# Batch 1 of a fused windowed-attention and feed-forward kernel split into two token groups, with the order of its loads, the trigger of w_out's last quarter and one attention group's key changed

## Chip, cores and metric

One core of one Trainium2 chip. The metric is the device time of one execution in microseconds (us), of the slowest core (here the only one). The four executions of the kernel before lie within 0.5% (229.15 to 230.26 us). A run is marked slow when it is over 1.5% above the fastest of its kernel; ratios use the other, "fast" runs alone. Profiles are of single executions; their span is about 1.7 us shorter than the time (229.87 against 228.2).

## The reference

```python
# q, k, v: (4, 8, 768, 64) = batch, heads, tokens, head size; n_sink = 4, window = 128
scores = q @ k.T / 8
keep   = (key < 4) | ((0 <= query - key) & (query - key < 128))
a      = softmax(where(keep, scores, -1e9))
x      = (a @ v), heads side by side            # (3072, 512)
g      = relu(x @ w_in) ** 2                    # w_in (512, 2048)
out    = g @ w_out                              # w_out (2048, 512)
```

So each batch has attention over a window of 128 keys plus 4 "sink" keys, and then two matrix products, called layer 1 and layer 2 here.

## The kernel before

The kernel plans itself: each operation has a key and a cost, a small planner in the program estimates start times and fixes one order for each engine; on the chip every engine runs its program in that order. What the change and the argument touch:

```python
sizes = dict(att=2, den=2, qr=5, qs=6, vf=3, expm=8, r=3, osb=2)   # buffers; att, den: PSUM
GROUPS = {b: [(0, 6)] for b in range(B)}            # first token, tiles of 128 tokens
GROUPS[0] = [(0, 2), (256, 2), (512, 2)]

def load_qk(b, m0, ti, g, ...):                     # on the SP queue: 4 heads of q or k
    ... in_=(q, k)[ti][b, 2*m0:2*m0+4, t0:t0+128*n, :].rearrange("h (p t) d -> p h (t d)", t=n)

# VectorE (or GpSimd): the four sink rows of v, spread over the heads; from 8 KB "vs_in"
def sink_values(e):
    for j in range(NP):
        tensor_tensor(out=vs[32*j:32*j+32, 2*j:2*j+2, :], in0=vs_in[:, b:b+1, :]..., op=mult)
# values (PE): needs the masks, the cast v tiles and sink_values; takes a PSUM buffer
# norm (VectorE): reciprocal and multiply out of that PSUM buffer, which is free after it
# layer1 (PE): takes a "den" buffer; relu (ACT), square (VectorE)
# layer2 of batch 0, tokens 0 to 511: goes through w_out by quarters and keeps both
#   "den" buffers until the fourth quarter is done
# attention of batch 0 and 1 may use both "att" and "den"

# order of the loads, from batch 1 on; load_w_out and the loads of batch 2 are on the POOL queue
for m0 in (0, 2):
    for ti in (1, 0):
        load_qk(1, m0, ti, 0, ...)                  # 4 x 768 KB
load_w_out(3, ("qk", 1, 0, 0, 0), ...)              # behind the first q load
for s in range(NS):
    load_v(1, s, ...)                               # 3 x 2 x 256 KB
for b in range(1, B):
    load_sinks("sp", b)                             # 8 KB each, last of all
# batch 2's first load waits for ("v", 1, 3), the fourth of batch 1's six v loads

at(2, 0.8, 1.3, "att")                              # batch 0's last attention group
attention(1, lambda f: -0.1 + 0.4 * f)(0, 0.0, 1.0, ("att", "den"))
```

The softmax here doesn't subtract the row's maximum and nothing guards it: scores larger than these inputs give would overflow.

Of the kernel before, what the change touches and what calls it, by code (L numbers as in the profile page):

```python
# [40 lines left out]
class Plan:  # L41
# [11 lines left out]
    def op(self, key, engines, run, after=(), takes=(), reads=(), dma=0.0, follow=()):  # L53
        o = Op(key, engines, run, after, takes, reads, dma, follow)
        self.ops.append(o)
        return o
# [77 lines left out]
def kernel(  # L134
# [17 lines left out]
    NS = NT // 2  # L152
# [127 lines left out]
    def dma_op(queue, name, run, us, behind=None, takes=(), yields=()):  # L280

        def go(e):
            ds = run(e)
            if behind is not None:
                for d in ds:
                    after_dma(d, loaded[behind])
            loaded[name] = ds[-1]
        o = op(-5, {queue: (0.85 if queue == "pool" else 0.5) + (0.3 if behind else 0.0)}, go, dma=us, takes=takes,
               follow=[chained[queue]] if queue in chained else (),
               after=[ops[behind]] if behind is not None else ())  # L290
        ops[name] = chained[queue] = o
        o.yields += [ops[y] for y in yields]
        o.follow += [ops[y] for y in yields]
        return o
# [9 lines left out]
    def load_w_out(i, behind=None, yields=()):  # L304
        w_out_op[i] = dma_op(
            "pool", ("w_out", i),
            lambda e: [nc.gpsimd.dma_start(
                out=w_out_sb[:, 4 * i:4 * i + 4, :],
                in_=moe_w_out[512 * i:512 * i + 512, :].rearrange("(p f) m -> p f m", p=128))],
            2.6, behind, yields=yields)  # L310
# [6 lines left out]

    GROUPS = {b: [(0, 6)] for b in range(B)}
    GROUPS[0] = [(0, 2), (256, 2), (512, 2)]
    ROW = {256: 0.0205, 512: 0.028, 1024: 0.046, 1536: 0.068}  # L320

    def load_qk(b, m0, ti, g, behind=None, yields=()):


        t0, n = GROUPS[b][g]
        half = (g if g < 2 else m0 // 2) if b == 0 else None
        share = (m0 if g < 2 else "g2", ti) if b == 0 else (b, m0, ti)
        if not half:
            qr_slot[share] = Slot("qr", 2)
        qr_slot[b, m0, ti, g] = qr_slot[share]  # L330

        def run(e):
            if b == 0:
                if half == 0:
                    qr_t[share] = work["qr"].tile([128, 2, 4, n * D], FP32, name="qr", tag="qr")
                t = qr_t[share][:, half]
            else:
                t = work["qr"].tile([128, 4, n * D], FP32, name="qr", tag="qr")
            qr_t[b, m0, ti, g] = t
            return [nc.sync.dma_start(  # L340
                out=t,
                in_=(q, k)[ti][b, 2 * m0:2 * m0 + 4, t0:t0 + 128 * n, :].rearrange(
                    "h (p t) d -> p h (t d)", t=n))]
        ops["qk", b, m0, ti, g] = dma_op("sp", ("qk", b, m0, ti, g), run, 32 * ROW[256 * n], behind,
                                         () if half else [qr_slot[share]], yields)

    def load_v(b, s, behind=None, yields=()):

        sl = vf_slot[b, s] = Slot("vf", 1)
        for i in range(2):  # L350
            t = 2 * s + i

            def run(e, i=i, t=t):
                if i == 0:
                    vf_t[b, s] = work["vf"].tile([128, 2, H, D], FP32, name="vf", tag="vf")
                return [nc.sync.dma_start(
                    out=vf_t[b, s][:, i], in_=v[b, :, 128 * t:128 * t + 128, :].rearrange("h p d -> p h d"))]
            dma_op("sp", ("v", b, t), run, 8 * 8 * ROW[256], behind if i == 0 else None,
                   [sl] if i == 0 else (), yields)
# [35 lines left out]
    def attention(b, key):  # L395
# [16 lines left out]
        def stage(g, f0, f1, side):  # L412

            t0, n = groups[g]
            last = t0 + 128 * n
# [6 lines left out]
            if b in NATURAL:  # L422
                for s in range(NS):
# [10 lines left out]
                            ops["turn", b, ti, t].margin = 4.0  # L434
                            copies.append(ops["turn", b, ti, t])
                    ops["cast", b, s] = ops["v", b, 2 * s + 1]
            w = 2 if b == 0 else 1
            for m in range(0, NP, w) if b not in NATURAL else ():
                f = 0.08 * m
                m0 = m - m % 2  # L440
# [245 lines left out]
    def layer1(b, key, fbs, c0, cw, need):  # L686
        n = len(fbs)
        xT = xT_sb[b % 2]
        bs, rs = Slot("den", 1), Slot("r", 1)
        tag = (b, fbs[0], c0)  # L690

        def mm(e):
            pm = bank_t[tag] = bank(bs, "pm", [128, n, cw], FP32)
            for i, fb in enumerate(fbs):
                for kb in range(NKB):
                    nc.tensor.matmul(pm[:, i, :], lhsT=w_in_sb[:, fb // 4, kb, fb % 4:512:4],  # L696
                                     rhs=xT[:, c0 // 256:(c0 + cw) // 256, kb, :], start=(kb == 0), stop=(kb == NKB - 1))
        a = op(key, {"pe": n * NKB * cw / 2380.0}, mm, takes=[bs],
               after=[ops["xT", b, s] for s in need] + [w_in_op[fbs[0] // 4]])
        ops["layer1", b, fbs[0], c0] = a  # L700

        def relu(e):
            r = bank_t[tag, "r"] = work["r"].tile([128, n, cw], BF16, name="r", tag="r")
            if e == "act":
                nc.scalar.activation(out=r, in_=bank_t.pop(tag), func=AF.Relu)  # L705
            else:
                nc.vector.tensor_scalar_max(r, bank_t.pop(tag), 0.0)
        ra = op(key, {"act": 0.19 + n * cw / 1200.0, "dve": 1.25}, relu, after=[a], takes=[rs], reads=[bs])

        def square(e):  # L710
            r = bank_t.pop((tag, "r"))
            (nc.vector if e == "dve" else nc.gpsimd).tensor_mul(  # L712
                gT_sb[c0 // 512][:, fbs[0]:fbs[0] + n, c0 % 512:c0 % 512 + cw], r, r)
        ops["sq", b, fbs[0], c0, cw] = op(key, {"dve": 0.7}, square, reads=[rs],
                                      after=[ra] + [ops[x] for x in ops if x[0] == "layer2" and x[1] == b - 1])
# [65 lines left out]
    for g, m0 in ((0, 0), (0, 2), (1, 0), (1, 2)):  # L781
        for ti in (1, 0):
            load_qk(0, m0, ti, g)
        if g:
            load_v(0, m0 // 2)
# [4 lines left out]
    for m0 in (0, 2):  # L790
        for ti in (1, 0):
            load_qk(0, m0, ti, 2, ("w_out", 0) if m0 == 0 and ti == 1 else None, [("w_out", 1)])
    load_v(0, 2)
    load_w_out(2, ("qk", 0, 2, 0, 2), [("v", 0, 5)])
    for m0 in (0, 2):
        for ti in (1, 0):
            load_qk(1, m0, ti, 0, ("qk", 0, 2, 0, 2) if m0 == 0 and ti == 1 else None, [("w_out", 2)])
    load_w_out(3, ("qk", 1, 0, 0, 0), [("qk", 1, 2, 0, 0)])
    for s in range(NS):
        load_v(1, s, yields=[("w_out", 3)] if s else ())  # L800
    for b in range(1, B):
        load_sinks("sp", b)

    LO, HI = 0.05, 0.6
    for b in range(B):
        if b == 0:
            at = attention(0, lambda f: f - 1.0)
            at(0, 0.0, 0.5, ("den", "att"))
            at(1, 0.5, 1.0, ("den", "att"))
            w_in_op[2].follow += [ops["cast", 0, 0]]  # L810
            w_out_op[0].follow += [ops["cast", 0, 1]]
            late["masks"] = op(-0.01, {"pool": 3.0}, build_masks, after=[c_tri, ops["bridge", 0, 1]])
            at(2, 0.8, 1.3, "att")
        if b == 0:
            for i in range(4):
                for s in range(2):
                    layer1(b, 0.083 * i + 0.042 * s, range(4 * i, 4 * i + 4), 256 * s, 256, (s,))
        else:
            for i, fb in enumerate(range(0, NFB, 2)):
                layer1(b, b + 0.333 * i / 8, (fb, fb + 1), 0, 512, (0, 1))  # L820
        for i, fb in enumerate(range(0, NFB, 4)):
            layer1(b, b + 0.333 + 0.167 * i / 4, range(fb, fb + 4), 512, 256, (2,))
        if b + 1 < B:
            if b + 1 in NATURAL:
                for s in range(NS):
                    load_natural(b + 1, s, [o for x, o in ops.items() if x[0] == "values" and x[1] == b - 1])
            attention(b + 1, (lambda f: -0.1 + 0.4 * f) if b == 0 else lambda f, b=b: b + LO + (HI - LO) * f)(
                0, 0.0, 1.0, ("att", "den") if b == 0 else "att")
        for u in range(NS):
            if b == 0 and u < 2:  # L830
                layer2(b, u, lambda i, part, u=u: 0.5 + 0.5 * (4 * part + 2 * u + i) / 24, by_part=True)
            else:
                layer2(b, u, lambda i, part, u=u, b=b: b + 0.5 + 0.5 * (8 * u + 4 * i + part) / 24)
# [36 lines left out]
```

## Time and profile before

| | before |
|---|---|
| time, median of the three first runs | 230.25 us |
| span of the profiled run | 228.2 us |
| TensorE (PE) busy | 216.7 us |
| PE idle 43.50 to 54.85 us | 2.73 us |
| PE idle 54.85 to 82.30 us | 1.20 us |
| batch 1's sink rows land | 58.80 us |

PE is the bound: all it does not do is 11.5 us. The prediction shows the lines for that. One more view matters later, VectorE's timeline (start, length, engine, line, operation, out<-in, shapes, count; in brackets the idle time before and who ended it):

```profile
59.06 0.70 DVE L208 CAST v<-vf 128x1024 bf16<-128x1024 f32 x1 [1.40 <-DMA vf<-in_v_dram]
59.67 2.37 DVE L519 TENSOR_TENSOR vs<-vs_in,head_rows 32x130 bf16<-32x130 f32 x8
62.16 0.69 DVE L712 TENSOR_TENSOR gT<-r 128x1024 bf16<-128x1024 bf16 x1
```

The second line is the work on the sink rows of batches 1 and 2. It has no bracket: the rows had landed 0.9 us before VectorE came to it.

### The profile page before, as it was taken

How to read it: one execution, taken by the hardware profiler on the slowest of the kernel's cores; microseconds unless marked ns; L12 is line 12 of the kernel's file. 1: busy time of each engine (PE TensorE's matmuls, PEld its weight loads, DVE VectorE, ACT ScalarE, POOL GpSimd, SP SyncE). 2: the span in 40 equal slices, each digit the busy share in tenths (PEclk: the TensorE clock that was granted, in tenths of full speed). 3: DMA queues.
4: the chain of work that ended last, by engine and by line, in shares of the span. 5: the costliest groups of instructions: out<-in, count | busy, mean ns of one | idle time of the engine just before them, and what ended most of it. 6: DMA issues, size and time to landing. Idle time of an engine off the chain costs nothing.

```text
span 228.2 us, 4562 instructions
## 1 busy us (share of the span) xinstructions
PE 216.7 (95%) x1923; PEld 138.2 (61%) x1940; DVE 105.3 (46%) x196; ACT 113.9 (50%) x127; POOL 56.4 (25%) x85
## 2 busy tenths in 40 slices
PE   7989999878999989999999999999999999999993
PEld 7558995455785665579545445488545455784441
DVE  6673444477775568575434015585532023440010
ACT  2496556344776478578260147768351056551010
POOL 5175016132986549766000000000000000000000
PEclk9999999999999999999999999999999999999999
DMA  5999989999999999999995630004061420000222
GB/s 158 269 201 206 215 207 261 309 320 218 174 197 142 141 201 137 142 123 146 156 138 152 174 115 3 0 0 49 0 122 38 120 95 0 0 0 3 92 94 92
DMA packets 84245, 29.70 MB, mean 130 GB/s; under 512 B 70272, under 2 KB 80768, under 8 KB 84224
## 3 DMA queue, kind: packets, MB, share of 16 engines
q0 software_dynamic: 40128, 8.92, 48.6%
q1 hardware_dynamic: 43912, 20.35, 41.2%
q8 instruction: 15, 0.25, 0.4%
q10 hardware_dynamic: 184, 0.14, 0.2%
q14 instruction: 6, 0.05, 0.1%
HBM read 27.30 MB, written 6.29 MB: 147 GB/s over the span
## 4 chain that ended last, share of the span: by engine, by line
PE 76%; DMA 10%; ACT 6%; DVE 4%; issue 1%; SPq 1%; ACTq 0%
PE pm L696 34%; PE py L736 32%; DMA qr<-in_q_dram 7%; PE po L636 5%; DMA w_out_sb<-in_moe_w_out_dram 4%; PE ps L575 4%; ACT r L705 4%; DVE gT L712 2%; ACT expm L594 1%; SPq L340 1%; PE px L673 1%; DVE qkT L208 1%; PE pk L535 1%; ACT qkT L206 1%; PE ps L568 0%
## 5 line engine op out<-in xcount | busy, mean ns | idle before, releaser
L696 PE MATMUL pm<-xT,w_in_sb 128*128 128x256 bf16 (+1 forms) x576 | 87.1, 309 | 0.5 <-ACT r L705 0.4
L736 PE MATMUL py<-w_out_sb,gT 128*128 128x512 bf16 x369 | 85.6, 379 | 2.0 <-DMA w_out_sb<-in_moe_w_out_dram 1.0
L696 PEld LDWEIGHTS <-w_in_sb 128*128 128x128 bf16 x576 | 62.7, 114 | 20.8 <-issue 2.1
L705 ACT ACTIVATE r<-pm 128x1024 bf16<-128x1024 f32 x48 | 49.3, 1027 | 32.2 <-PE pm L696 24.2
L736 PEld LDWEIGHTS <-gT 128*128 128x128 bf16 x384 | 36.1, 98 | 42.0 <-issue 2.4
L712 DVE TENSOR_TENSOR gT<-r 128x1024 bf16<-128x1024 bf16 x48 | 33.7, 701 | 55.3 <-ACT r L705 55.2
L594 ACT ACTIVATE expm<-ps 128x1024 bf16<-128x1024 f32 (+1 forms) x48 | 43.2, 955 | 12.5 <-PE ps L575 12.4
L206 ACT ACTIVATE osb<-py 128x1024 f32<-128x1024 f32 x11 | 11.3, 1025 | 45.4 <-PE py L736 45.4
L603 DVE TENSOR_TENSOR expm<-expm,mask 128x1024 bf16<-128x1024 bf16 (+1 forms) x38 | 25.0, 668 | 17.5 <-ACT expm L594 16.9
L636 PEld LDWEIGHTS <-expm 128*128 128x128 bf16 x352 | 16.5, 97 | 5.8 <-issue 1.8
L636 PE MATMUL po<-v,expm 128*128 128x65 bf16 x352 | 17.7, 193 | 2.0 <-DVE qkT L208 1.2
L648 DVE TENSOR_TENSOR xn_sb<-po,rc 128x512 bf16<-128x512 f32 x24 | 16.6, 691 | 1.1 <-DVE rc L647 0.3
L575 PE MATMUL ps<-qkT 64*128 64x128 bf16 (+1 forms) x256 | 14.8, 238 | 0.4 <-DVE xn_sb L648 0.2
L575 PEld LDWEIGHTS <-qkT 64*128 64x128 bf16 x256 | 8.0, 94 | 9.9 <-issue 8.0
L636 PE MATMUL po<-vs,es 128*128 128x65 bf16 x128 | 13.1, 193 | 0.0
L206 ACT ACTIVATE qkT<-pt 128x512 bf16<-128x512 bf16 (+1 forms) x11 | 7.2, 674 | 11.6 <-PE pt L472 9.8
L647 DVE RECIPROCAL rc<-po 128x8 f32<-128x8 f32 x24 | 4.9, 205 | 16.9 <-PE po L636 16.8
L210 POOL CAST qs<-qr 128x512 bf16<-128x512 f32 (+1 forms) x8 | 6.0, 750 | 24.2 <-DVE gT L712 12.3
L373 POOL DMA_DIRECT2D qn<-in_q_dram x12 | 10.8, 906 | 3.8 <-DMA qn<-in_k_dram 3.7
L636 PEld LDWEIGHTS <-es 128*128 128x128 bf16 x128 | 11.7, 97 | 0.0
L373 POOL DMA_DIRECT2D qn<-in_k_dram x12 | 10.7, 898 | 2.9 <-DMA vf<-in_v_dram 1.6
L383 POOL DMA_DIRECT2D v<-in_v_dram x12 | 10.6, 888 | 2.5 <-DMA qn<-in_q_dram 1.9
(50 smaller groups left out, 93.0 us busy)
## 6 DMA issues: line engine op xcount, KB each, us to landing
out_dram<-osb SPq DMA_DIRECT2D x11, 512.0 KB, 3.0
vf<-in_v_dram SPq DMA_DIRECT2D x12, 256.0 KB, 5.2
w_in_sb<-in_moe_w_in_dram POOLq DMA_DIRECT2D x4, 512.0 KB, 8.1
w_out_sb<-in_moe_w_out_dram POOLq DMA_DIRECT2D x4, 512.0 KB, 10.9
qr<-in_k_dram SPq DMA_DIRECT2D x6, 256.0 KB, 4.4
qr<-in_q_dram SPq DMA_DIRECT2D x6, 256.0 KB, 4.5
qr<-in_k_dram SPq DMA_DIRECT2D x2, 768.0 KB, 8.0
qr<-in_q_dram SPq DMA_DIRECT2D x2, 768.0 KB, 9.6
```

The lines of the kernel that those rows point to most:

```text
L206: nc.scalar.activation(out=dst, in_=src, func=AF.Copy)
L373: return [nc.gpsimd.dma_start(out=qn_t[b, ti][:, t, :].rearrange("p (h d) -> p h d", d=D), in_=(q, k)[ti][b, :, 128 * t:128 * t + 128, :]. ...
L383: return [nc.gpsimd.dma_start(out=v_sb[b % 2][:, t, :, 0:D], in_=v[b, :, 128 * t:128 * t + 128, :].rearrange("h p d -> p h d"))]
L575: nc.tensor.matmul(ps[:, h2, o:o + w], lhsT=qkT_sb[r, m, 1, c, :], rhs=qkT_sb[r, m, 0, qb:qb + w // 128, :], start=(i == 0 and not biased) ...
L594: nc.scalar.activation(out=x[:, :, o:512], in_=bank_t["s", b, s, m][:, :, o:512], func=AF.Exp, scale=scale)
L603: nc.vector.tensor_mul(x[:, :, o:512], x[:, :, o:512], mk[:, :, o:512])
L636: nc.tensor.matmul(pv[:, i, h2, :], lhsT=lhsT, rhs=rhs, start=(n_ == 0), stop=(n_ == len(mms) - 1))
L648: nc.vector.tensor_tensor(out=xn_sb[:, 2 * s:2 * s + 2, 128 * m0:128 * m0 + 256].rearrange("p i (j h d) -> p j i h d", j=2, d=D), in0=pv[: ...
L696: nc.tensor.matmul(pm[:, i, :], lhsT=w_in_sb[:, fb // 4, kb, fb % 4:512:4], rhs=xT[:, c0 // 256:(c0 + cw) // 256, kb, :], start=(kb == 0), ...
L705: nc.scalar.activation(out=r, in_=bank_t.pop(tag), func=AF.Relu)
L712: (nc.vector if e == "dve" else nc.gpsimd).tensor_mul(gT_sb[c0 // 512][:, fbs[0]:fbs[0] + n, c0 % 512:c0 % 512 + cw], r, r)
L736: nc.tensor.matmul(pm[:, i, :], lhsT=gT_sb[t // 4][:, fb, 128 * (t % 4):128 * (t % 4) + 128], rhs=w_out_sb[:, fb, :], start=(fb == 0), sto ...
```

## The change

The intent: batch 1's first 512 tokens no longer wait for the loads and transposes of its last 256, so that TensorE gets attention work sooner; batch 0's last group is put earlier; the fourth quarter of w_out is released behind the third load of the new first group.

```diff
--- before.py
+++ after.py
@@ -317,20 +317,25 @@
 
     GROUPS = {b: [(0, 6)] for b in range(B)}
     GROUPS[0] = [(0, 2), (256, 2), (512, 2)]
+    GROUPS[1] = [(0, 4), (512, 2)]
     ROW = {256: 0.0205, 512: 0.028, 1024: 0.046, 1536: 0.068}
 
     def load_qk(b, m0, ti, g, behind=None, yields=()):
 
 
         t0, n = GROUPS[b][g]
-        half = (g if g < 2 else m0 // 2) if b == 0 else None
-        share = (m0 if g < 2 else "g2", ti) if b == 0 else (b, m0, ti)
+        if b == 0 and g < 2:
+            half, share = g, (b, m0, ti)
+        elif n == 2:
+            half, share = m0 // 2, (b, "last", ti)
+        else:
+            half, share = None, (b, m0, ti)
         if not half:
             qr_slot[share] = Slot("qr", 2)
         qr_slot[b, m0, ti, g] = qr_slot[share]
 
         def run(e):
-            if b == 0:
+            if half is not None:
                 if half == 0:
                     qr_t[share] = work["qr"].tile([128, 2, 4, n * D], FP32, name="qr", tag="qr")
                 t = qr_t[share][:, half]
@@ -434,7 +439,7 @@
                             ops["turn", b, ti, t].margin = 4.0
                             copies.append(ops["turn", b, ti, t])
                     ops["cast", b, s] = ops["v", b, 2 * s + 1]
-            w = 2 if b == 0 else 1
+            w = 2 if n == 2 else 1
             for m in range(0, NP, w) if b not in NATURAL else ():
                 f = 0.08 * m
                 m0 = m - m % 2
@@ -795,9 +800,13 @@
     for m0 in (0, 2):
         for ti in (1, 0):
             load_qk(1, m0, ti, 0, ("qk", 0, 2, 0, 2) if m0 == 0 and ti == 1 else None, [("w_out", 2)])
-    load_w_out(3, ("qk", 1, 0, 0, 0), [("qk", 1, 2, 0, 0)])
-    for s in range(NS):
-        load_v(1, s, yields=[("w_out", 3)] if s else ())
+    load_v(1, 0)
+    load_w_out(3, ("qk", 1, 2, 1, 0), [("v", 1, 1)])
+    load_v(1, 1, yields=[("w_out", 3)])
+    for m0 in (0, 2):
+        for ti in (1, 0):
+            load_qk(1, m0, ti, 1)
+    load_v(1, 2)
     for b in range(1, B):
         load_sinks("sp", b)
 
@@ -810,7 +819,7 @@
             w_in_op[2].follow += [ops["cast", 0, 0]]
             w_out_op[0].follow += [ops["cast", 0, 1]]
             late["masks"] = op(-0.01, {"pool": 3.0}, build_masks, after=[c_tri, ops["bridge", 0, 1]])
-            at(2, 0.8, 1.3, "att")
+            at(2, 0.55, 0.75, "att")
         if b == 0:
             for i in range(4):
                 for s in range(2):
@@ -824,8 +833,12 @@
             if b + 1 in NATURAL:
                 for s in range(NS):
                     load_natural(b + 1, s, [o for x, o in ops.items() if x[0] == "values" and x[1] == b - 1])
-            attention(b + 1, (lambda f: -0.1 + 0.4 * f) if b == 0 else lambda f, b=b: b + LO + (HI - LO) * f)(
-                0, 0.0, 1.0, ("att", "den") if b == 0 else "att")
+            if b == 0:
+                at = attention(1, lambda f: -0.1 + 0.4 * f)
+                at(0, 0.0, 0.7, ("att", "den"))
+                at(1, 0.7, 1.0, ("att", "den"))
+            else:
+                attention(b + 1, lambda f, b=b: b + LO + (HI - LO) * f)(0, 0.0, 1.0, "att")
         for u in range(NS):
             if b == 0 and u < 2:
                 layer2(b, u, lambda i, part, u=u: 0.5 + 0.5 * (4 * part + 2 * u + i) / 24, by_part=True)
```

## The prediction

> **What bounds the kernel now.** I read the page's busy shares first, then the chain that ended last, then the windows and the timeline of TensorE (PE) where the chain leaves it, and last the waits.
>
> ```profile
> PE 216.7 (95%) x1923; PEld 138.2 (61%) x1940; DVE 105.3 (46%) x196; ACT 113.9 (50%) x127; POOL 56.4 (25%) x85
> ```
>
> PE is busy 216.7 of 228.2 us, so all of its idle time is 11.5 us. No change that leaves the matmuls as they are can win more than a part of that. The windows split it at the places where the chain changes (us, then PE busy, weight loads, DVE, ACT, POOL, granted clock, DMA share, GB/s):
>
> ```profile
> 34.20:43.50 9.30, 9.16 (x70) 4.50 (x70) 4.22 (x7) 5.34 (x7) 3.43 (x5) 1.00 1.03 258
> 43.50:54.85 11.35, 8.62 (x118) 5.95 (x119) 8.69 (x14) 3.91 (x6) 3.54 (x5) 1.00 1.11 300
> 54.85:82.30 27.45, 26.25 (x297) 18.04 (x299) 18.40 (x40) 18.72 (x22) 18.11 (x21) 1.00 1.72 168
> 82.30:228.20 145.90, 141.02 (x1071) 83.03 (x1080) 55.09 (x94) 66.85 (x72) 19.37 (x24) 1.00 0.70 83
> ```
>
> Idle (length less busy): 0.14, 2.73, 1.20 and 4.88 us. The last row is mostly the end: PE's last matmul ends near 224.3, which leaves 3.9 us of copies and stores that the change does not touch. The rest, 11.5 - 0.14 - 2.73 - 1.20 - 4.88 = 2.5 us, lies before 34.2, where the change moves nothing. So the change works on **2.73 + 1.20 = 3.93 us**. The chain of waits shows what ends the first of them:
>
> ```profile
> 36.56 9.60 DMA qr<-in_q_dram
> 46.16 0.29 issue
> 46.45 8.34 DMA w_out_sb<-in_moe_w_out_dram
> 54.79 0.04 issue
> 54.83 0.38 PE py L736
> ...
> 81.65 0.61 DVE xT L208
> 82.26 0.05 issue
> 82.31 1.92 PE pm L696 x8
> ```
>
> The fourth quarter of w_out may start only behind the first q load of batch 1 (landed 46.16) and lands at 54.79; PE waits for it. The second idle stretch ends when the transposed activations of batch 1, tokens 256 to 511, are copied (82.26): layer 1 of batch 1 needs tokens 0 to 511 and nothing else is left. PE's timeline shows the holes one by one (brackets: idle before, and who ended it):
>
> ```profile
> 44.00 1.02 PE L736 MATMUL py<-w_out_sb,gT 128*128 128x512 bf16 x4 [0.54 <-DMA w_out_sb<-in_moe_w_out_dram]
> 51.34 0.22 PE L636 MATMUL po<-v,expm 128*128 128x65 bf16 x2 [1.22 <-DVE qkT L208]
> 53.51 0.84 PE L472 MATMUL pt<-ident,qs 128*128 128x128 bf16 x12 [0.48 <-DVE xn_sb L648]
> 54.83 1.02 PE L736 MATMUL py<-w_out_sb,gT 128*128 128x512 bf16 x3 [0.47 <-DMA w_out_sb<-in_moe_w_out_dram]
> ```
>
> The 1.22 us hole is a PSUM buffer: the second half of batch 0's last attention waits until the copies of batch 1's 768-column transposes leave one of the two "att" buffers. The other two buffers ("den") are held by layer 2 of batch 0 from 34 us until w_out is complete, so layer 1 of batch 0's last 256 tokens cannot fill the holes either.
>
> **What the Trainium skill says.** (1) "DMA: Bandwidth & Descriptors", section "Queues, rings and completion order": each DMA engine takes turns between the queues with work, packet by packet. The trace agrees only in part: the w_out load issued at 46.45 landed after 8.34 us, and the packets of its queue ended almost all after 51 us, when the backlog of the other queue had drained; so bytes issued before its trigger count in full. (2) "Perfetto Trace Analysis", section "DMA Optimizations": larger pieces use the memory better, and splitting lets some of the data start earlier. Both sides show here: 397 GB/s in 44 to 46 us with 1536-byte rows, 261 in 34 to 36 us with 512-byte rows. (3) The same page, section "Optimizing Scalar/DVE Operations": each operation has a fixed part of some 60 to 125 ns on DVE, 51 to 93 on ACT, in engine time. The trace agrees roughly: DVE copies of transposes take 955 ns for 768 columns and 688 for 512, which leaves 154 ns at zero columns; ACT 810 and 596, which leaves 168.
>
> **The change, part by part.**
>
> (a) Bytes. Batch 1's q and k arrive as four loads of 512 KB (1024-byte rows) and later four of 256 KB (512-byte rows), before four of 768 KB. The fourth quarter of w_out now waits for the third load, so the data ahead of the trigger are 3 x 512 KB = 1.5 MB against 2 x 768 KB: the same. Behind it in the queue stood two more loads and a v tile, 2.0 MB; now one load and v, some 1.0 to 1.3 MB. I therefore estimate the landing 0 to 1.5 us earlier than 54.79. The 1 MB in 512-byte rows costs 1/0.261 - 1/0.397, or 1.3 us more DMA time (estimate from the two windows), but at the end of the input queue, where only tokens 512 to 767 of batch 1 and the small sink rows wait for it.
>
> (b) Instructions. 96 transposes before and after. Casts of q and k: 8 of 768 columns become 8 of 512 and 4 of 512; copies of transposes the same. That is 4 more of each, by about 0.1 and 0.16 us: about 1 us, spread over DVE, ACT and POOL, which are 46, 50 and 25% busy. The sink scores of batch 1 become two groups of four of 256 columns for one of 512. They pipeline at 0.33 us for four of 512 and 0.22 for four of 256 in the chain, so +0.11 us of PE. On the path: **+0.1 us**.
>
> (c) PSUM holding times. A batch 1 transpose held an att buffer for 0.67 (PE) + 0.81 (ACT) + 0.96 (DVE), about 2.4 us, as the DVE copy follows the ACT copy; with 512 columns it is 0.45 + 0.60 + 0.69 = 1.74. And batch 0's last attention group is put at an earlier key (0.55 to 0.75 in place of 0.8 to 1.3), ahead of batch 1. So the 1.22 and 0.48 us holes should go.
>
> (d) What can fill PE until w_out is complete. From 34.2 to 54.83 PE did 20.6 - 2.85 = 17.8 us of work. New to that stretch are batch 0's last bridge (8 transposes, 0.45 us in the chain) and the first scores of batch 1 (8 matmuls in 0.44, twice, for the first 256 tokens, 0.9 us in all), which were at 61 and 65 us. That is 1.35 us, to which an earlier landing may add up to 1. I count **-1.7 us**, and leave 1.0 us of the 2.73.
>
> (e) The end of batch 1's first 512 tokens. Their values need the sink rows of v, loaded last of all (issued at 55.7, and used by DVE from 59.67 for 2.37 us). That load does not come earlier, by (a) even 1 us later. The chain from there (values at 65.49, layer 1 at 82.31) has less in its way, because scores, masks and copies of the last 256 tokens come after it; but those also filled PE until 82. I take **-0.5 us** of the 1.20.
>
> (f) Loads of batch 2 wait for the second v tile of batch 1, now ahead of the last q and k in the queue, so they start some 3 us sooner, in company with these. After 82 us PE has no wait on a load above 0.2 us, so I give this 0 to +0.2 us.
>
> Sum: +0.1 - 1.7 - 0.5 + 0.1 = -2.0 us, and 230.25 - 2.0 = **228.2 us**.
>
> **The rivals.** *All holes close.* Then 3.9 us less 0.1: 226.4. For it: PE would have layer 1 and layer 2 work for every hole after 55 us. Against it: den is held until w_out is complete, and (d) finds too little other work before that. A gain over 2%, 4.6 us, would need more than all idle time in reach. *The wait moves.* The sink rows and v come later behind slower 512-byte rows and the loads of batch 2, the first 512 tokens are ready no sooner than 82 us, and PE, which has its other work done sooner, waits there for what it saved before: 230 to 230.5. For it: 16.8 us lie between the first values and layer 1 in the profile before, with DVE and ACT busy two thirds of that stretch. Against it: the chain has fewer operations in between. *The order goes wrong.* Engines run in program order, fixed from estimated landings. The loads of batch 2 in front of, or beside, the last q and k could hold POOL, which casts both, and then PE: 231 to 235. The profile before speaks neither way; POOL is 18 of 27 us busy after 55.
>
> **Range and chances.** The middle is between the first two rivals. 226.2 is all holes closed and a little; 230.9 is the moved wait with a fault of half a us. Chances: faster by over 2% (below 225.65) 0.06, as it needs more than the idle time in reach; slower by over 2% 0.06, the third rival; within 2% 0.88.
>
> **What would show it right or wrong.** Right: PE busy within 0.5 us of 216.7; the fourth quarter of w_out landing at 53 to 55; no PE wait on a copy of transposes near 51; idle of about 1 us before that landing and below 1 us from there to layer 1 of batch 1; that layer beginning near 80. Wrong: a PE wait above 1 us at layer 1 of batch 1 or at its last 256 tokens (second rival); POOL waiting for a landing with PE behind it (third); or w_out landing later than 56, since more than my sum counts then stands ahead of it.

## The result

The change made the kernel slower: 236.44 us median in four runs (235.56, 235.92, 236.96 and one slow run of 373.98), against 230.14 us before. The ratio of the fast runs is **1.027** (95% interval 1.022 to 1.032). Ratios here are the mean time of one kernel's fast runs over that of the other's of the same rounds, so not quite the ratio of the medians. A second set of runs on another occasion gave 234.33 us and 1.020 (1.016 to 1.024). The prediction was 228.2 us, range 226.2 to 230.9.

The page of the profiled run (span 233.9 us) and the same windows as in the prediction:

```profile
PE 218.9 (94%) x1925; PEld 138.5 (59%) x1944; DVE 105.7 (45%) x197; ACT 114.5 (49%) x130; POOL 56.8 (24%) x89
```

```profile
34.20:43.50 9.30, 8.79 (x70) 4.46 (x70) 4.33 (x7) 4.57 (x6) 4.20 (x6) 1.00 0.89 217
43.50:54.85 11.35, 9.72 (x117) 6.12 (x118) 7.21 (x14) 5.20 (x8) 4.38 (x6) 1.00 1.09 259
54.85:82.30 27.45, 22.04 (x242) 15.65 (x242) 16.89 (x34) 16.83 (x21) 18.61 (x24) 0.88 2.00 187
82.30:233.90 151.60, 146.93 (x1139) 85.95 (x1147) 58.36 (x100) 68.77 (x74) 17.70 (x23) 1.00 0.64 82
```

PE's idle time in the second window fell as intended, from 2.73 to 1.63 us. In the third it rose from 1.20 to 5.41 us, and the granted clock there fell to 0.88. The chain that ended last (start, length, what) goes through this place:

```profile
57.37 7.39 DMA vs_in<-in_v_dram
64.76 0.02 issue
...
67.92 0.70 DVE xn_sb L653
68.62 0.05 issue
68.67 3.60 PE pm L701 x16
72.27 1.31 PE po L641 x24
```

An 8 KB load, the sink rows of batch 1, was issued at 57.37 and landed at 64.76 us, 6 us later than before. VectorE's timeline shows what that did:

```profile
60.71 1.02 DVE L608 TENSOR_TENSOR expm<-expm,mask 128x768 bf16<-128x768 bf16 x2
64.79 1.51 DVE L524 TENSOR_TENSOR vs<-vs_in,head_rows 32x130 bf16<-32x130 f32 x4 [3.06 <-DMA vs_in<-in_v_dram]
66.33 0.84 DVE L208 CAST v<-vf 128x1024 bf16<-128x1024 f32 x1
67.09 0.68 DVE L208 COPY qkT<-pt 128x512 bf16<-128x512 bf16 x1
67.69 0.19 DVE L652 RECIPROCAL rc<-po 128x8 f32<-128x8 f32 x1
67.92 0.69 DVE L653 TENSOR_TENSOR xn_sb<-po,rc 128x512 bf16<-128x512 f32 x1
```

VectorE stood 3.06 us for the rows. Behind the work on them came, in program order, the cast of the last v tile, a copy, and only then the normalisation (L652, L653) of attention values whose matmuls had ended near 64 us. That normalisation empties a PSUM "den" buffer, and the next to take one is layer 1 of batch 0's last 256 tokens (four groups of 16 matmuls on 256 columns, the first at 59.60 us). So PE stood too, 4.55 us, at work of batch 0; layer 1 of batch 1, on 512 columns, came only at 88.50 us (82.31 before):

```profile
68.67 3.60 PE L701 MATMUL pm<-xT,w_in_sb 128*128 128x256 bf16 x16 [4.55 <-DVE xn_sb L653]
```

And when it went on, it did so at half speed, here called the half clock. In windows of 2 us (length, then PE, weight loads, DVE, ACT, POOL, **granted clock**, DMA share, GB/s):

```profile
66.00:68.00 2.00, 0.00 (x0) 0.00 (x0) 1.94 (x5) 0.14 (x1) 1.85 (x4) 0.66 1.36 314
68.00:70.00 2.00, 1.33 (x7) 0.94 (x8) 1.97 (x5) 0.46 (x1) 2.00 (x3) 0.50 1.60 161
70.00:72.00 2.00, 2.00 (x11) 1.40 (x10) 1.26 (x2) 0.00 (x0) 1.83 (x3) 0.50 1.97 112
72.00:74.00 2.00, 2.00 (x38) 1.83 (x36) 0.34 (x2) 1.02 (x1) 0.00 (x0) 0.64 1.79 151
```

Sixteen layer-1 matmuls took 3.60 us in the chain, where sixteen of the same shape took 1.75 before; 24 value matmuls took 1.31 where they took 0.73. That is 1.85 + 0.58 = 2.43 us. With the wait, 4.55 + 2.43 = **7.0 us** were lost at this one place. The two spans differ by 233.9 - 228.2 = 5.7 us; so outside it, the changed kernel was some 1.3 us quicker. PE's busy time went up by 2.2 us, which is of the size of what the half clock took.

The half clock is something that the Trainium skill tells: "TensorE: Matmul & The Clock Gate", Part 1, says that TensorE's clock drops to half after an idle window of about 3.4 us and returns after as long a busy one, and that the window runs freely. The traces agree on the window's length. In the clock records of this trace the clock fell at 66.6 us, while PE was still waiting and only 2.5 us after its last matmul had ended (64.12), and came back at 73.4: 6.8 us, two windows. In e10 below it was down for 6.8 us too, in e4 for 3.4. They do not agree that the window must be idle: in the 3.41 us before the fall PE had been busy for 0.53 us here and for 1.61 us in e4. My prediction did not use that page.

### The profile page after: what moved, and what is told of

Same layout as the page of the kernel before. It is cut to its first block, busy times and chain, and to the rows that moved or that the text cites. A ratio compares the mean times of both kernels' runs of the same rounds, so it can differ in the third digit from the quotient of the medians.

```text
span 233.9 us, 4581 instructions
## 1 busy us (share of the span) xinstructions
PE 218.9 (94%) x1925; PEld 138.5 (59%) x1944; DVE 105.7 (45%) x197; ACT 114.5 (49%) x130; POOL 56.8 (24%) x89
## 4 chain that ended last, share of the span: by engine, by line
PE 69%; DMA 17%; SPq 7%; POOL 3%; DVE 2%; issue 1%; ACT 0%; POOLq 0%
PE pm L701 30%; PE py L741 29%; DMA w_out_sb<-in_moe_w_out_dram 6%; PE po L641 5%; DMA qr<-in_k_dram 4%; SPq L345 4%; DMA vf<-in_v_dram 4%; PE ps L580 3%; DMA vs_in<-in_v_dram 3%; SPq L361 3%; POOL w_in_sb L300 1%; PE px L678 1%; POOL qs L210 1%; DVE vs L524 1%; POOL v L210 0%
## 5 line engine op out<-in xcount | busy, mean ns | idle before, releaser
L701 PE MATMUL pm<-xT,w_in_sb 128*128 128x256 bf16 (+1 forms) x576 | 89.0, 313 | 4.9 <-DVE xn_sb L653 4.6
L717 DVE TENSOR_TENSOR gT<-r 128x1024 bf16<-128x1024 bf16 x48 | 33.2, 692 | 53.0 <-ACT r L710 53.0
L608 DVE TENSOR_TENSOR expm<-expm,mask 128x1024 bf16<-128x1024 bf16 (+1 forms) x39 | 25.6, 662 | 18.4 <-ACT expm L599 17.6
L206 ACT ACTIVATE osb<-py 128x1024 f32<-128x1024 f32 x10 | 10.2, 1023 | 38.1 <-PE py L741 30.5
L641 PEld LDWEIGHTS <-expm 128*128 128x128 bf16 x352 | 17.1, 99 | 4.9 <-issue 1.2
L653 DVE TENSOR_TENSOR xn_sb<-po,rc 128x512 bf16<-128x512 f32 x24 | 16.6, 691 | 0.8
L206 ACT ACTIVATE qkT<-pt 128x512 bf16<-128x512 bf16 x13 | 7.6, 598 | 14.2 <-PE pt L477 8.2
L641 PE MATMUL po<-vs,es 128*128 128x65 bf16 x128 | 13.7, 196 | 0.0
L652 DVE RECIPROCAL rc<-po 128x8 f32<-128x8 f32 x24 | 4.9, 204 | 16.8 <-PE po L641 16.7
L210 POOL CAST qs<-qr 128x512 bf16<-128x512 f32 x10 | 6.7, 672 | 22.6 <-DVE gT L717 12.3
L208 DVE COPY osb<-py 128x1024 f32<-128x1024 f32 (+2 forms) x3 | 2.3, 780 | 21.3 <-PE py L741 18.2
```

Of the source, the lines that this page charges most:

```text
L206: nc.scalar.activation(out=dst, in_=src, func=AF.Copy)
L608: nc.vector.tensor_mul(x[:, :, o:512], x[:, :, o:512], mk[:, :, o:512])
L641: nc.tensor.matmul(pv[:, i, h2, :], lhsT=lhsT, rhs=rhs, start=(n_ == 0), stop=(n_ == len(mms) - 1))
L653: nc.vector.tensor_tensor(out=xn_sb[:, 2 * s:2 * s + 2, 128 * m0:128 * m0 + 256].rearrange("p i (j h d) -> p j i h d", j=2, d=D), in0=pv[: ...
L701: nc.tensor.matmul(pm[:, i, :], lhsT=w_in_sb[:, fb // 4, kb, fb % 4:512:4], rhs=xT[:, c0 // 256:(c0 + cw) // 256, kb, :], start=(kb == 0), ...
L717: (nc.vector if e == "dve" else nc.gpsimd).tensor_mul(gT_sb[c0 // 512][:, fbs[0]:fbs[0] + n, c0 % 512:c0 % 512 + cw], r, r)
```

## The experiments

The theories:

- **A.** The late sink rows. They land 4 to 6 us later (62.81 in e10 and 64.76 after, against 58.80), VectorE waits for them in program order, PE waits for VectorE, and its clock falls.
- **B.** The last q, k and v as such, or their short rows, hold VectorE; the sink rows only land among them.
- **C.** The new order of operations (the earlier key above all) is worse by itself.

In the first five of the runs below with their own edit (e1 to e4 and e9), a comparison of the compiled programs showed the order of the compute work on every engine to be that of the kernel they were made from; only the loads named differ. In the others with an edit the planner made a new order. Twelve runs were made, all with three rounds against the kernel before, on four chips; ratios are to the runs of before on the same chip. The medians are of all runs, so those of e3 and e12 hold one slow run each, that of e11 two and that of e5 three.

| run | made from | median us | ratio to before (95%) |
|---|---|---|---|
| e10, unaltered | after | 234.33 | 1.020 (1.016 to 1.024) |
| e1, sink rows at the start | after | 230.74 | 1.003 (0.997 to 1.009) |
| e2, sink rows at the start | before | 229.78 | 1.000 (0.997 to 1.002) |
| e3, sink rows late | before | 233.55 | 1.013 (1.007 to 1.019) |
| e4, batch 2 behind the last v load | after | 231.68 | 1.005 (1.000 to 1.011) |
| e9, 2048-byte rows, wrong result | after | 234.39 | 1.019 (1.015 to 1.023) |
| e7, key alone | before | 231.89 | 1.010 (1.007 to 1.013) |
| e11, old key | after | 234.00 | 1.019 (1.016 to 1.022) |
| e5, sink rows at the start, planned | after | 236.75 | none |
| e6, as e5, and the last v tile sooner | after | 231.76 | 1.009 (1.006 to 1.013) |
| e8, as e5, and batch 2 later | after | 229.96 | 1.000 (0.997 to 1.004) |
| e12, as e8, with the old key | after | 233.43 | 1.014 (1.009 to 1.019) |

### e1: the changed kernel with early sink rows

```diff
-  vs_in rows of batch 1: SP queue, after all of batch 1's q, k and v
+  vs_in rows of batch 1: ACT queue, right behind batch 0's, at the start
```

> The changed kernel with one difference: the 8 KB of sink rows of batch 1 are loaded at the start, on the queue that loads batch 0's, and not last of all on the other queue. Every engine's program is the same, only that load moves. Theory A (the sink rows landed at 64.76 us, 6 us later than before, VectorE waits for them in program order, and TensorE behind it waits 4.55 us and then runs at half clock for some 5 us, which costs another 2.4): the next thing that VectorE needs is the last v tile of batch 1 (landed 63.24), so TensorE starts at about 65.5 in place of 68.67 and its clock does not fall: 236.2 - 3.1 - 2.4 = 230.7 us, range 229.5 to 231.5. Theory B (the bytes of the last q, k and v are what holds VectorE, the rows only land among them): 235 to 236, with the wait put down to the v tile. Theory C (the new order of operations is worse by itself): over 233, and the TensorE wait stays at over 3 us.

Measured: 230.74 us (229.34 to 232.10), where A said 230.7 and B and C over 233. The profiled run (229.71 us, span 228.0, clock 0.999), VectorE and then PE:

```profile
61.07 1.23 DVE L536 TENSOR_TENSOR vs<-vs_in,head_rows 32x130 bf16<-32x130 f32 x4
62.79 0.70 DVE L208 CAST v<-vf 128x1024 bf16<-128x1024 f32 x1 [0.49 <-DMA vf<-in_v_dram]
```

```profile
64.98 1.94 PE L713 MATMUL pm<-xT,w_in_sb 128*128 128x256 bf16 x16 [1.30 <-DVE xn_sb L665]
```

The wait on the rows is gone, PE's wait fell from 4.55 to 1.30 us, and sixteen matmuls take their usual 1.9 us in this view. The order of operations is the changed one throughout, so C is not what costs over 2%. Of B there remains 0.49 us, the wait for the last v tile. The four runs lie in two pairs, 229.3 and 229.7, 231.8 and 232.1. Their difference, 2.4 us, is the size of one fall of the clock, and the slower two had a mean granted clock of 0.992 and 0.991 against 0.999 and 0.997 (3.4 us at half clock take 0.0075 off the mean of 228 us). But only a quick one was profiled, so where the clock fell is not shown: in e6 and e8 below means of 0.992 and 0.993 came from the start of the kernel.

### e2: the kernel before with early sink rows, a control

> The kernel before, with the sink rows of batch 1 loaded at the start: a control. Its rows landed at 58.80 and VectorE used them at 59.67 without a wait, so theories A and B expect no change: 229.5 to 230.5 us, within 0.3% of before. A gain above 1% would say that the early load does something else as well.

Measured: 229.78 us, ratio 1.000. Loading the rows early does nothing where they were in time. PE's idle time from 43.50 to 54.85 us was 1.70 us in this run, and 1.89 in e3, with PE's order that of the kernel before: the 2.73 that my prediction started from was at the high end.

### e3: the kernel before with late sink rows

```diff
-  vs_in rows of batch 1: SP queue, last
+  vs_in rows of batch 1: POOL queue, behind the first load of batch 2
```

> The kernel before, with the sink rows of batch 1 loaded late: right behind the first load of batch 2 on that queue, to land at about 64 to 66 us in place of 58.8. The order on every compute engine is the same. Theory A: late rows alone are enough; VectorE waits from 59.7 to about 65, TensorE stands for 2 to 4 us and its clock falls: 232.5 to 237 us. Theory B and C: no more than 1 us, 230 to 231.

Measured: 233.55 us (231.67 to 235.75). The highest is marked slow (clock 0.985); the three fast runs are 1.3% slower than before. The median of the fast runs, 232.59, is within what A expected, and all of them are above what B and C did, though the lowest, 231.67, is below A's range as well. VectorE's and PE's lines:

```profile
64.60 2.37 DVE L526 TENSOR_TENSOR vs<-vs_in,head_rows 32x130 bf16<-32x130 f32 x8 [3.33 <-DMA vs_in<-in_v_dram]
```

```profile
68.22 0.82 PE L643 MATMUL po<-v,expm 128*128 128x65 bf16 x12 [2.10 <-DVE expm L610]
```

Without anything else of the change, 8 KB that land at 64.6 in place of 58.8 us cost 1.3%. The profiled run (232.59) kept its full clock, so in it the waits alone did this.

### e4: the changed kernel with batch 2's loads later

```diff
-  first load of batch 2 waits for ("v", 1, 3)
+  first load of batch 2 waits for ("v", 1, 5)
```

> The changed kernel with the first load of batch 2 waiting for the last v load of batch 1 in place of the fourth of six. Order on every engine the same. If the loads of batch 2 beside the last q, k and v of batch 1 are what makes the sink rows late (they began to move at 59 us), the last v tile lands near 61 and the rows near 61.5 to 62, TensorE waits under 1.5 us with its clock whole: 229.5 to 231 us. If the rows are late only by the bytes in front of them (1.5 MB behind the fourth quarter of w_out in place of 0.75 MB), they still land after 63.5 and the time stays over 233.

Measured: 231.68 us (229.31 to 232.24). The rows landed at 62.53 us and VectorE used them with no wait that the profile names, PE waited 1.42 us. The time is 0.7 us above the expected range. In the profiled run (232.24 us) the clock fell all the same, for 3.4 us; but that is not the whole reason, since another run took 231.94 us with a mean clock of 1.000:

```profile
66.01 3.54 PE L704 MATMUL pm<-xT,w_in_sb 128*128 128x256 bf16 x16 [1.42 <-DVE xn_sb L656]
```

```profile
64.00:66.00 2.00, 0.52 (x12) 0.40 (x11) 1.97 (x5) 1.52 (x3) 2.00 (x3) 0.98 0.79 247
66.00:68.00 2.00, 1.99 (x10) 1.41 (x11) 1.97 (x5) 0.00 (x0) 2.00 (x3) 0.50 1.93 123
```

So the company of batch 2's loads is part of why the rows are late. To size it, take the time from the issue of batch 1's first k load to the landing of the rows, out of the traces, one profile each (us):

| kernel | issue | rows land | between |
|---|---|---|---|
| before | 36.10 | 58.80 | 22.7 |
| e7 (before, key alone) | 37.10 | 59.92 | 22.8 |
| after | 36.95 | 64.76 | 27.8 |
| e10 (after again) | 35.89 | 62.81 | 26.9 |
| e9 (after, long rows) | 37.31 | 64.96 | 27.7 |
| e4 (after, batch 2 later) | 37.13 | 62.53 | 25.4 |

The change delays the rows by 4.2 to 5.1 us; 1.5 to 2.4 of these are batch 2's loads. The other 2.7 us are not explained by an experiment. What the traces show is that at 48 us, with the fourth quarter of w_out on its way, SP had issued all but three v loads (0.75 MB) of batch 1 before the change, and all but four q and k and two v loads (1.5 MB) after it, in both cases followed by the rows. That those 0.75 MB are the 2.7 us fits, but is argued only.

### e10 and e9: the changed kernel again, and with long rows

```diff
-  last q, k of batch 1: 512-byte rows
+  last q, k of batch 1: as many bytes in 2048-byte rows, from other places (wrong result)
```

> The changed kernel once more, unaltered, as the base of this batch: 235 to 237.5 us, with the sink rows of batch 1 landing at 63.5 to 66 us, a TensorE wait of 3.5 to 5.5 us and a clock at half for about 5 us behind it.

> The changed kernel with a wrong result on purpose: the four 256 KB loads of the last q and k of batch 1 read as many bytes in rows of 2048 bytes in place of 512. If the short rows are what makes the queue behind them slow (my prediction gave them 1.3 us), the last v tile and the sink rows land 1 to 3 us earlier than in the unaltered changed kernel of this batch, and the time is 1 to 5 us shorter. If the row size does not matter, the rows land within 0.5 us of that kernel's and the time is the same.

Measured: 234.33 us for e10 (just below its range, with PE waiting 3.4 us at the same place and the clock at 0.50 from 65.4 to 72.2 us) and 234.39 for e9, whose rows land no sooner (27.7 us against 26.9). The length of the rows is not the cause; this part of B falls, and with it the 1.3 us that my prediction gave to them.

### e7 and e11: the key alone, and the change without it

```diff
 e7 (before):   - at(2, 0.8, 1.3, "att")     + at(2, 0.55, 0.75, "att")
 e11 (after):   - at(2, 0.55, 0.75, "att")   + at(2, 0.8, 1.3, "att")
```

> The kernel before with one part of the change alone: the earlier key of batch 0's last attention group. The loads keep their order, so the sink rows land near 59 and no wait of over 1.3 us should appear: 229 to 230.5 us by theory A. If the order of operations that the key makes is to blame (theory C), 232 or more.

> The changed kernel with one part undone: the key of batch 0's last attention group as before. Loads as in the change. Theory A: the sink rows still land at 62.5 to 65 us, VectorE waits for them in program order (the four operations on them now stand behind the last v tile), so there is still a TensorE wait of over 1.5 us with a clock fall: 232 to 236 us. Theory C (the key, which alone cost 1% in the kernel before, is the main cause): 230 to 231.5, with no wait on the rows that TensorE sees.

Measured: e7 231.89 us, 1% slower than before, in neither theory's range, though within 0.1 us of C's: the key costs something by itself with the old loads, in small waits (the longest 0.9 us) that no single cause explains. e11 stays 1.9% slower, so taking the key out does not mend the change. In its one profiled run (231.45 us, the quickest of six) VectorE waited 4.2 us in two places for v tiles and 0.3 us for the rows, which now come behind the last tile in its program, and PE 2.1 us behind it. So in that order the v tile is as much the wait as the rows. The other runs of e11 had a mean clock of 0.985 or 0.993 against 0.999 in the profiled one; what they lost by it no profile shows.

### e5, e6, e8 and e12: looking for a better version

```diff
 e5:  + sink rows of batch 1 at the start, known to the planner
 e6:  e5, and load_v(1, 2) ahead of the last q and k of batch 1
 e8:  e5, and the first load of batch 2 behind ("v", 1, 5)
 e12: e8, and at(2, 0.8, 1.3, "att")
```

> The changed kernel with the sink rows of batch 1 loaded at the start and known to the planner, which now puts the four operations on them into VectorE's idle time near the start. What still stands in VectorE's program before the normalisation is the mask and no longer the last v tile, so the 1.3 us wait of the first early-rows run should shrink below 0.6 us with the clock whole: 228 to 229.5 us, 0.3 to 0.8% faster than the kernel before. If the new order meets another wait, 230 to 232.

> A candidate: the changed kernel with the sink rows of batch 1 at the start, and the last v tile of batch 1 ahead of its last q and k. The v tile is no longer in the way of the normalisations, but the last q and k land some 2 us later: 228 to 229.5 us; over 231 if VectorE now waits for q and k instead.

> A candidate: the changed kernel with the sink rows of batch 1 at the start and the loads of batch 2 behind the last v load of batch 1, both known to the planner. No TensorE wait over 0.6 us between 50 and 82 us: 228 to 229.5 us.

> A candidate: sink rows of batch 1 at the start, loads of batch 2 behind the last v load of batch 1, and the old key, all known to the planner; so of the change there remain the two groups of batch 1 and the order of w_out and v. If the key was all that was still wrong, 228 to 229.5 us, faster than the kernel before by 0.3 to 0.8%; if batch 1 in two groups is worth nothing by itself, 229.5 to 231.

None beats the kernel before, and all four missed the gain they were made for. But they carry a cost of their own. The planner, told that batch 1's rows are there early, put VectorE's four operations on them in front of its first casts of q and k. VectorE and then PE at the start, before and in e8:

```profile
4.15 1.18 DVE L519 TENSOR_TENSOR vs<-vs_in,head_rows 32x130 bf16<-32x130 f32 x4 [0.37 <-POOL tri L222]
```

```profile
3.96 2.95 DVE L524 TENSOR_TENSOR vs<-vs_in,head_rows 32x130 bf16<-32x130 f32 x8 [0.19 <-DMA vs_in<-in_v_dram]
7.42 0.52 PE L477 MATMUL pt<-ident,qs 128*128 128x128 bf16 x6 [2.05 <-DVE qs L208]
```

Before, PE had no such wait. In e8 the clock then fell to 0.50 from 7.8 to 11.2 us, and the first layer-2 matmul started at 36.07 us, in e6 at 36.23; before at 34.19, in e1 at 34.06. So e8 (229.62 to 230.64) equals the kernel before although its profiled run, the slowest of the four, was 1.9 us behind at that point. What the two groups of batch 1 are worth with both causes of the wait mended is therefore open; e1's order with e4's edit would tell, and was not run. e6 is 0.9% slower, 2.1 us by the medians, and was 2.0 us behind at that point; near the last q and k of batch 1 VectorE waited 1.1 us for a k load, and PE at most 0.8 us at a time. e12 is 1.4% slower by its fast runs (232.36 to 234.44), so the old key does not help here; why is open, as its profile is of a run marked slow. e5 gave 232.40 to 237.81 us with one fast run of four, and I read nothing further from it.

## Why the prediction was wrong, by its steps

- **What bounds the kernel** (PE, with 3.93 us of idle time in reach): right that PE bounds it, but the 2.73 us of one profile was 1.70 and 1.89 in two other runs of that order. There was less to win than I counted.
- **(a) Bytes.** The landing of the fourth quarter was right (53.78 us, estimated 53.3 to 54.8). The price of short rows (1.3 us) was wrong: e9 shows none. It came from a misread window: by the packet records, the 261 GB/s of 34 to 36 us were 252 KB of q and k in 512-byte packets and 255 KB of v in 256-byte ones, so not the rate of 512-byte rows.
- **(b) Instructions.** Right: four more matmuls, as the weight loads show (1940 before, 1944 after; PE's own records, 1923 and 1925, are incomplete). PE's busy time rose 2.2 us, mostly by the half clock. The fixed parts that the prediction read from the trace (154 ns on DVE, 168 on ACT) are of copies out of PSUM; the page named there has about 125 and 51 for these, so it fits roughly for DVE only.
- **(c) PSUM holding times.** Right: the 1.22 us wait on a copy of transposes is gone (0.2 left), though a wait of 0.6 on a normalisation came at the bridge (the transposes of the attention's output).
- **(d) Filling.** In direction right: 1.63 us of idle time left where I said 1.0.
- **(e) The sink rows.** This is the step that failed. It says of their load "by (a) even 1 us later" and takes -0.5 us for the stretch. Counted from the issue of batch 1's first load, they came 4.2 to 5.1 us later. I had seen that the values need them, and had their landing as a margin of 0.9 us in the timeline before. I did not ask what else stands behind them in VectorE's fixed order: normalisations that free the PSUM buffer layer 1 takes. Nor did I see that this buffer is wanted by layer 1 of batch 0, the very work that was to fill PE until layer 1 of batch 1. In place of -0.5 the runs showed a PE wait of 3.4 to 4.55 us (e10, after) there. e1 takes the rows out and 3.6 us of the median go with it, against e10, which ran on another chip; against before on their own chips, 1.020 falls to 1.003. e3 puts the same lateness into the kernel before and gets 1.3% slower; there PE waited for masked exponentials behind the rows in VectorE's program (L610), not for that buffer.
- **(f) Batch 2's loads.** "0 to +0.2 us" looked at waits after 82 us only. Beside the end of batch 1's queue they delay the rows by 1.5 to 2.4 us (e4).
- **A term that the sum did not have:** the clock. 2.43 us in the profile after.
- **The rivals.** The second named the loads, and that the wait moves to them, but put it at layer 1 of batch 1 (82 us) and capped it at 230.5 us: it let PE wait only for what it had saved. The wait came at layer 1 of batch 0's last tokens (64 to 69 us). The third, 231 to 235, came nearest in the number (236.44 at first, 234.33 in e10) and put it on POOL's casts; it was VectorE.

## What to carry to other kernels

When a change reorders a queue, look at the last small load in it, at how much margin its user had, and at everything behind that user on an engine that runs in order; the price is that of the engine's whole program, not of the load. A wait of the tensor engine costs more than its length when it lets the clock fall. And one profile's idle time is not yet the gain to be had: take it from more than one run. When the planner is told of a mend, look at the start of the kernel too: e5, e6 and e8 paid for the early rows there.

## What the Trainium skill lacked or had wrong

- "TensorE: Matmul & The Clock Gate", Part 1: the page ties the half clock to an idle window of about 3.4 us and the full one to a busy window. The length fits: in the clock records of the 14 profiles every stretch between two changes is a whole multiple of 3.413 us. "Idle" and "busy" do not. Laying windows of 3.41 us from these changes, the clock fell after windows with PE busy for 0 to 47% (47% in e4, behind a wait of 1.42 us), and kept full speed after windows with 52% and more, and once with 45% (e5, at the start). At half clock it stayed there after 40, 65 and 70% and came back after 80% and more. The page has no such shares, nor what one fall costs in a kernel with full PE otherwise (2.43 us after the change).
- "DMA: Bandwidth & Descriptors", section "Latency and other measured facts": the page gives about 0.6 us to the first byte of such a load. Behind a filled queue, an 8 KB load took 7.39 us from issue to landing after the change and 3.1 us before. The page has no time for a small load behind a queue.
- "Perfetto Trace Analysis", section "DMA Optimizations": larger rows were worth nothing here (e9 234.39 us, e10 234.33) for the last 1 MB of batch 1's q and k, in rows of 2048 in place of 512 bytes.
- No page has a case like this one, where a late small load holds up other operations through the order of one engine's program, with its price: 8 KB landing 5.8 us later cost 1.3% (e3).
